# Attention of the first four units with float32 products, and ten products for each norm

## The chip, the cores and the metric

The kernel runs on one core of a Trainium2 chip. A core has five engines that run beside each other and wait for one another by semaphores: TensorE (PE, matrix products; its weight loads are listed as PEld), VectorE (DVE), ScalarE (ACT), GpSimd (POOL) and SyncE (SP, which issues the transfers). The metric is the time of one execution on the device in microseconds (us); of several runs the median is given.

## The reference

Attention over 4 batches of 8 heads with 576 positions and 64 columns, mixed with the read of a memory, then two feed-forward blocks over 2304 tokens of 512 columns:

```python
scores = scale * np.matmul(q, k.transpose(0, 1, 3, 2))   # causal mask, softmax -> a
local = np.matmul(a, v)
q_p = phi(q)                                             # x + 1 above 0, exp(x) below
mem_ret = np.einsum('bhsd,bhde->bhse', q_p, M_prev)
mem_norm = np.einsum('bhsd,bhd->bhs', q_p, z_prev)[..., None] + 1e-06
x = g * mem_ret / mem_norm + (1 - g) * local             # g from beta
x = silu(x @ moe_w_in) @ moe_w_out                       # 512 -> 2048 -> 512
h = x @ moe2_w_in                                        # 512 -> 1024
solu = h * softmax(h)
out = (layer norm of solu, times g_ln) @ moe2_w_out      # 1024 -> 512
```

All inputs are float32, and the result has to be near float32.

## The kernel before

Products are made with the type float32r (F32R), which keeps fewer bits. So every operand is split in two parts, a high one (a cast) and a low one (what the cast left off), and a product is a sum of three: high by high, low by high, high by low. ACT makes the casts, DVE or POOL subtracts for the low parts.

The work is cut into 16 units, each a pair of heads of one batch; units 0 to 3 (u < NN = 4) are batch 0. A unit goes through these steps, each a function:

- load_qk, split_both (units 0 to 3) or load_head, split_head (the others): q and k come in as rawqk; split_both makes qkh and qkl of them.
- scores: nine tiles t for a unit, 0 to 3 for the first head, 5 to 8 for the second, 4 for the last 64 queries of both. For units 0 to 3 a tile takes three products into pss: qkh by qkh, qkl by qkh, qkh by qkl.
- softmax_max (DVE, into a and nm), softmax_exp (ACT), transposes (PE, into pst).
- t_hi and t_lo: pst is written to SBUF as aTh (ACT, a cast) and aTl (DVE, a subtraction). Both are one buffer for all units.
- load_v, split_v: V comes as rawv and is split into vhl, for each head the high part beside the low part (128 columns).
- av: for each head and stretch of queries, products of vhl with aTh and aTl by key block kb into psav; the two halves of psav are added (ACT copies one into xs, DVE adds the other). The last key block has 64 rows.
- load_m, phi: the memory (rawm) is split into mh, phi of q (phe) into phh and phl. norm makes psn, 3 products for each 128 queries, so 15 for a unit of 576, and rn from it; mem makes psm with three products and y. products and spread (psr) lay factors out, finish puts the unit's output into x (POOL).

Units 0 to 3 are done in two turns each, first queries 0 to 255 of all four, then 256 to 575 of all four; the others in one turn of 576. Between them the kernel loads and decodes six chunks of feed-forward weights (load_w: twelve pieces, each a transfer wraw into a single buffer, then ACT, three DVE instructions wf, an ACT cast and a POOL subtraction into w), and it fills PE with the feed-forward work of finished batches (fill_h into psh, fill_y into psfy). The rest of the first block (psh, psy) and the second (psh, pso) follow.

The order is not that of the code. Every call is recorded with a due position (DUE, T_1, T_2, T_0), and plan (lines 240 to 313) plays them through with a table of costs (length, lines 209 to 238) and puts out one order for all engines; issue then gives the instructions in that order, so nearly all of them have line 358 in a profile, and one goes by the names of the tiles. While PE would stand idle in the first 100 us of that play, transposes of the identity named warm are put in (idle, line 1076). Buffers come from rings (p1 to p4 hold 1 to 4 buffers for a tag): a new tile of a tag waits until the one that many before it is finished.

## Time and profile before

| | |
|---|---|
| time before, median of 3 runs | 965.91 us (958.58 to 969.98) |
| the profiled execution: its own time | 966.33 us |
| its span, from the first to the last instruction | 964.5 us |
| mean granted clock of TensorE | 0.977 of full |
| PE busy | 912.0 us, 95% |
| DVE busy | 631.1 us, 65% |
| ACT busy | 508.3 us, 53% |
| POOL busy | 436.6 us, 45% |

The profile is of one execution. An engine is busy while it runs an instruction; matrix products are pipelined, and their ends are modelled, so their durations overlap and a busy PE need not be at its peak. What a product costs in a row of many is best read from the time of the whole row, divided by their number. The chain of waits follows the work that ended last back from the end, at each step to what released it. "issue" in it is time in which an engine waited for nothing that the profile shows.

### The profile page before, as it was taken

Reading aid. Unit: us, or ns where it says so; the run is one execution under the profiler, and the core shown is the slowest. Engines: PE = TensorE matmul, PEld = TensorE weight load, DVE = VectorE, ACT = ScalarE, POOL = GpSimd, SP = SyncE. Lnnn points to the kernel's source line nnn. Section 1 sums busy time; section 2 is a strip of 40 time slices with the busy share of each in tenths; the row PEclk is TensorE's granted clock in tenths of the full one; section 3 lists DMA queues with packets and bytes.
Section 4 is the critical chain, followed back from the end, with each engine's and each line's share of the span. In section 5 each row is a group of like instructions: output and inputs, shape, how many; then the busy total and the mean of one; then the engine's idle time right before and its main releaser. Section 6 shows DMA issues by size and latency. Waiting matters only on the chain.

```text
span 964.5 us, 16266 instructions
## 1 busy us (share of the span) xinstructions
PE 912.0 (95%) x5956; PEld 837.5 (87%) x5956; DVE 631.1 (65%) x1448; ACT 508.3 (53%) x1221; POOL 436.6 (45%) x366
## 2 busy tenths in 40 slices
PE   7889889999999999999978999799899999999998
PEld 5668779998999999999878999799898888888886
DVE  6887886886877675715698323953536766666663
ACT  5655578986877776745555324443434233333322
POOL 5865688776876755433454123442533211111100
PEclk9987799999999999999999999999999999999999
DMA  4433344333333221045434201320000000000000
GB/s 116 132 103 99 117 136 153 96 118 127 105 103 92 95 85 34 7 151 235 133 119 135 68 1 28 113 80 1 1 1 1 12 23 23 22 23 23 22 22 34
DMA packets 26655, 72.00 MB, mean 75 GB/s; under 512 B 3152, under 2 KB 10064, under 8 KB 25680
## 3 DMA queue, kind: packets, MB, share of 16 engines
q1 hardware_dynamic: 26576, 70.97, 22.9%
q8 instruction: 47, 0.77, 0.4%
q14 instruction: 32, 0.26, 0.1%
HBM read 60.34 MB, written 10.62 MB: 74 GB/s over the span
## 4 chain that ended last, share of the span: by engine, by line
PE 71%; DVE 17%; ACT 4%; issue 4%; DMA 2%; POOL 1%; SPq 0%; ACTq 0%; DVEq 0%; POOLq 0%
PE psh L358 24%; PE psy L358 10%; PE pso L358 10%; DVE wf L358 8%; PE psav L358 6%; PE psfy L358 6%; PE pst L358 5%; PE pss L358 5%; PE psr L358 2%; PE psn L358 2%; DMA wraw<-in_w 2%; DVE aTl L358 1%; ACT wf L358 1%; DVE phe L358 1%; PE psm L358 1%
## 5 line engine op out<-in xcount | busy, mean ns | idle before, releaser
L358 PE MATMUL psh<-xh,w 128*128 128x288 f32 (+2 forms) x1024 | 203.8, 299 | 2.6 <-ACT w L358 1.7
L358 PEld LDWEIGHTS psh<-xh,w 128*128 128x128 f32 x1024 | 160.8, 189 | 4.3 <-ACT w L358 1.9
L358 POOL TENSOR_TENSOR xl<-x,xh 128x1152 fp32r<-128x1152 f32 (+3 forms) x35 | 88.2, 2522 | 115.5 <-ACT xh L358 108.5
L358 PE MATMUL psh<-xl,w 128*128 128x288 f32 (+2 forms) x512 | 139.8, 301 | 0.0
L358 DVE TENSOR_TENSOR glo<-psh,gh 128x288 fp32r<-128x288 f32 (+2 forms) x128 | 57.7, 452 | 123.3 <-ACT gh L358 123.0
L358 PE MATMUL psy<-gh,w 128*128 128x288 f32 x736 | 117.7, 298 | 8.1 <-DVE y L358 4.7
L358 PEld LDWEIGHTS psy<-gh,w 128*128 128x128 f32 x736 | 104.6, 189 | 11.4 <-ACT gh L358 4.2
L358 POOL TENSOR_TENSOR w<-wf,w 128x512 fp32r<-128x512 f32 x48 | 66.9, 1395 | 94.9 <-ACT w L358 94.7
L358 PE MATMUL pso<-w,tb 128*128 128x512 f32 x432 | 104.0, 397 | 0.0
L358 ACT ACTIVATE a<-a,nm 128x128 f32<-128x128 f32 (+4 forms) x144 | 84.4, 588 | 24.2 <-DVE nm L358 22.2
L358 PEld LDWEIGHTS pso<-w,tb 128*128 128x128 f32 x432 | 79.9, 188 | 17.2
L358 PEld LDWEIGHTS psh<-xl,w 128*128 128x128 f32 x512 | 92.5, 191 | 0.9 <-issue 0.8
L358 DVE SCALAR_TENSOR_TENSOR wf<-wraw,wf 128x512 uint32<-128x512 uint32 x96 | 90.9, 947 | 3.0
L358 PE MATMUL psh<-w,yh 128*128 128x512 f32 x288 | 90.2, 394 | 0.0
L358 DVE TENSOR_TENSOR aTl<-pst,aTh 128x512 fp32r<-128x512 f32 (+4 forms) x160 | 75.3, 483 | 22.0 <-ACT aTh L358 21.2
L358 DVE CUSTOM_DVE_ANT_0 a<-pss,tri 128x128 f32<-128x128 f32 (+4 forms) x144 | 67.0, 477 | 23.0 <-PE pss L358 18.8
L358 ACT CAST aTh<-pst 128x512 fp32r<-128x512 f32 (+4 forms) x160 | 65.7, 424 | 27.0 <-PE pst L358 24.4
L358 PE MATMUL pst<-ident,a 128*128 128x128 f32 (+1 forms) x400 | 72.8, 288 | 6.1 <-DVE aTl L358 4.4
L358 PE MATMUL psy<-glo,w 128*128 128x288 f32 x368 | 67.4, 298 | 11.1 <-DVE glo L358 11.0
L358 ACT ACTIVATE psh<-psh 128x288 f32<-128x288 f32 x84 | 33.1, 395 | 73.5 <-PE psh L358 73.5
L358 PE MATMUL psfy<-gh,w 128*128 128x288 f32 (+2 forms) x288 | 66.2, 311 | 1.5 <-ACT w L358 1.1
L358 PE MATMUL psav<-aTh,vhl 128*128 128x320 f32 (+4 forms) x224 | 65.8, 306 | 0.6 <-ACT aTh L358 0.5
(118 smaller groups left out, 2050.2 us busy)
## 6 DMA issues: line engine op xcount, KB each, us to landing
wraw<-in_w SPq DMA_DIRECT2D x32, 512.0 KB, 3.8
rawqk<-in_qk SPq DMA_DIRECT2D x24, 608.0 KB, 3.8
rawv<-in_vp SPq DMA_DIRECT2D x16, 320.0 KB, 3.0
...
```

Of the source, the lines that this page charges most:

```text
L358: getattr(target, method)(*[real(a) for a in args], **{k: real(v) for k, v in kw.items()})
```

## The change

For units 0 to 3 nothing is split any more. split_both passes rawqk on, and a tile of scores takes one float32 product. split_v passes rawv on: a product with V takes both heads' 128 columns at once, and one of them replaces the two with aTh and aTl. phi and mem use rawm and phe as they are, norm takes one product for each 128 queries, mem one instead of three. t_lo does nothing for these units; the one float32 copy of pst is made by ACT for tiles 0 to 4 and by DVE for 5 to 8. av then needs one ACT copy of psav and no addition.

Buffers: rawqk comes from the ring "st" of three. aTh and aTl become rings: units 0 to 3 use them by turns as two float32 buffers (named aTh and aTl by turns), from unit 4 on they are again the high and the low part. rawv of units 0 to 3 takes the tags "rawv" and "vhl" by turns, and rawm gets two buffers.

For the other units norm has ten products instead of 15: phh and phl each by four columns of mh, and DVE adds the two column pairs. The last key block is multiplied on 128 rows instead of 64 in all units; its lower rows are zeroed by an ACT copy once for each of the four buffers. The planner gets a price for float32 products, and the order is planned anew.

```diff
--- before.py
+++ after.py
@@ -222,6 +222,8 @@
             if method == "transpose":
                 return 109, 0
             m = cols(shape(args[1]))
+            if args[1].ap.dtype == F32:
+                return max(n, m) / .6, 0
             if m == 64:
                 return (n if o.offset < 64 * o.ap[0][0] else 128) / 2.4, 0
             return max(n, 2 * m) / 2.4 + 2.5, 0
@@ -510,9 +512,20 @@
 
     UP, LOW = slice(0, 64), slice(64, 128)
     first_q = {}
+    st = {}
     heads, raws, v_t, mem_t, s_t, unit, X, Xd, Yd = {}, {}, {}, {}, {}, {}, {}, {}, {}
-    aTh = p1.tile([128, 4096], F32R, name="aTh")
-    aTl = p1.tile([128, 4096], F32R, name="aTl")
+    a_t = {}
+
+    def a_of(u, n=0):
+
+
+        n = ("f", turn_of[u] % 2) if u < NN else ("r", n)
+        if n not in a_t:
+            a_t[n] = p1.tile([128, 3840], F32 if u < NN else F32R, tag=f"aT{n[1]}", name="aT" + "hl"[n[1]])
+
+            act.copy(heads_of(a_t[n])[64:128, :, 1024:1088], tri[64:128, 0:128].rearrange("p (j q) -> p j q", j=2))
+        return a_t[n]
+
 
     def early(u, q1, tag, tags):
 
@@ -523,7 +536,7 @@
 
         n = q1 - q0
         if u < NN:
-            raw = p2.tile([128, QW], F32, tag="rawqk", name="rawqk")
+            raw = p3.tile([128, QW], F32, tag="st", name="rawqk")
             if q1 < S:
                 sp.dma_start(raw[:, 0:2 * n].rearrange("p (t s) -> p t s", t=2),
                              qk[u, :, 0:2 * S].rearrange("p (t s) -> p t s", t=2)[:, :, 0:n])
@@ -546,14 +559,9 @@
 
     def split_both(u, q1):
         raw = raws.pop(u)
-        n = raw.shape[1]
-        hi = p3.tile([128, QW], F32R, tag="st", name="qkh")[:, 0:n]
-        lo = p3.tile([128, QW], F32R, tag="st", name="qkl")[:, 0:n]
-        act.copy(hi, raw)
-        pool.tensor_tensor(lo, raw, f32(hi), ALU.subtract)
-        k, q = slice(0, q1), slice(q1, n)
+        k, q = slice(0, q1), slice(q1, raw.shape[1])
         for j, r in enumerate((UP, LOW, slice(0, 128))):
-            heads[u, j] = [(hi[r, q], hi[r, k]), (lo[r, q], hi[r, k]), (hi[r, q], lo[r, k])]
+            heads[u, j] = [(raw[r, q], raw[r, k])]
 
     def split_head(u, j):
 
@@ -568,33 +576,41 @@
 
     def load_v(u, q1):
         n = (q1 + 127) // 128
-        raws["v", u] = p1.tile([128, 5, 2, 64], F32, tag="rawv", name="rawv")[:, 0:n]
+        st["v"] = st.get("v", 0) + (u < NN)
+        raws["v", u] = p1.tile([128, 5, 2, 64], F32, tag="vhl" if u < NN and st["v"] % 2 else "rawv", name="rawv")[:, 0:n]
         sp.dma_start(raws["v", u], vp[u, :, 0:n].rearrange("p c (j d) -> p c j d", j=2))
 
     def split_v(u, q1):
         raw = raws.pop(("v", u))
+        if u < NN:
+            v_t[u] = raw.rearrange("p c j d -> p c (j d)")
+            return
         vhl = p1.tile([128, 5, 2, 128], F32R, tag="vhl", name="vhl")[:, 0:(q1 + 127) // 128]
         dve.tensor_copy(vhl[:, :, :, 0:64], raw)
         pool.tensor_tensor(vhl[:, :, :, 64:128], raw, f32(vhl[:, :, :, 0:64]), ALU.subtract)
         v_t[u] = vhl
 
     def load_m(u):
-        rm = p1.tile([128, 2, 132], F32, tag="rawm", name="rawm")
+        rm = p2.tile([128, 2, 132], F32, tag="rawm", name="rawm")
         sp.dma_start(rm, mz[u // 2])
         for n in range(2):
             raws["m", u + n] = rm[:, n]
 
     def phi(u, q0, q1):
         rq, rm = raws.pop(("q", u)), raws.pop(("m", u))
-        mhl = p2.tile([128, 262], F32R, tag="mh", name="mh")
-        dve.tensor_copy(mhl[:, 0:132], rm)
-        pool.tensor_tensor(mhl[:, 132:262], rm[:, 0:130], f32(mhl[:, 0:130]), ALU.subtract)
+        if u >= NN:
+            mhl = p2.tile([128, 262], F32R, tag="mh", name="mh")
+            dve.tensor_copy(mhl[:, 0:132], rm)
+            pool.tensor_tensor(mhl[:, 132:262], rm[:, 0:130], f32(mhl[:, 0:130]), ALU.subtract)
         n = q1 - q0
         k = early(u, q1, S, [320] * NP)
         e = p1.tile([128, k], F32, tag=early(u, q1, "phe", ["g", "phe", "g", "phe"]), name="phe")[:, 0:n]
         dve.tensor_scalar(e, rq, 0.0, None, ALU.min)
         act.activation(e, e, AF.Exp)
         dve.scalar_tensor_tensor(e, rq, 0.0, e, ALU.max, ALU.add)
+        if u < NN:
+            mem_t[u] = (rm, e)
+            return
         ph = p1.tile([128, k], F32R, tag=early(u, q1, "phh", ["gh0", "gh1", "gh2", "gh3"]), name="phh")[:, 0:n]
         pl = p1.tile([128, k], F32R, tag=early(u, q1, "phl", ["gl0", "gl1", "gl2", "gl3"]), name="phl")[:, 0:n]
         dve.tensor_copy(ph, e)
@@ -632,34 +648,45 @@
 
     def norm(u, q0, q1):
 
-        mhl, ph, pl = mem_t[u]
+        of = mem_t[u]
         n = q1 - q0
         starts = [min(c, n - 128) for c in range(0, n, 128)]
         k = len(starts)
-        ps = ps_a.tile([128, 5, 2], F32, tag="av", name="psn")[:, 0:k]
+        ps = ps_a.tile([128, 5, 4], F32, tag="av", name="psn")[:, 0:k]
+        rn = p2.tile([128, 5, 2], F32, tag="rn", name="rn")[:, 0:k]
         order.chain = []
         for i, c in enumerate(starts):
             c = slice(c, c + 128)
-            for m, (x, z) in enumerate(((ph, 130), (ph, 132), (pl, 130))):
-                pe.matmul(ps[:, i], x[:, c], mhl[:, z:z + 2], start=(m == 0), stop=(m == 2))
+            if u < NN:
+                pe.matmul(ps[:, i, 0:2], of[1][:, c], of[0][:, 0:2], start=True, stop=True)
+            else:
+                pe.matmul(ps[:, i], of[1][:, c], of[0][:, 130:134], start=True, stop=False)
+                pe.matmul(ps[:, i], of[2][:, c], of[0][:, 130:134], start=False, stop=True)
         order.chain = None
-        rn = p2.tile([128, 5, 2], F32, tag="rn", name="rn")[:, 0:k]
-        dve.tensor_scalar(rn, ps, 1e-6, None, ALU.add)
+        if u < NN:
+            dve.tensor_scalar(rn, ps[:, :, 0:2], 1e-6, None, ALU.add)
+        else:
+            dve.tensor_scalar(rn, ps[:, :, 2:4], 1e-6, None, ALU.add)
+            dve.tensor_tensor(rn, ps[:, :, 0:2], rn, ALU.add)
         dve.reciprocal(rn, rn)
         g = g8[:, 2 * (u % NP):2 * (u % NP) + 2].unsqueeze(1).broadcast_to([128, k, 2])
         unit["rmb", u] = products(rn, g), None
 
     def mem(u, q0, q1):
-        mhl, ph, pl = mem_t.pop(u)
-        mh, ml = mhl[:, 2:130], mhl[:, 134:262]
+        of = mem_t.pop(u)
         rmb = unit.pop(("rmb", u))
         n = q1 - q0
         y2 = p1.tile([128, early(u, q1, S, [320] * NP)], F32, tag=early(u, q1, "y2", ["gh4", "gl4", "y2", "gh4"]), name="y2")[:, 0:n]
         for cs in cuts(n):
             ps = ps_a.tile([128, cs.stop - cs.start], F32, tag="av", name="psm")
-            pe.matmul(ps, mh, ph[:, cs], start=True, stop=False)
-            pe.matmul(ps, ml, ph[:, cs], start=False, stop=False)
-            pe.matmul(ps, mh, pl[:, cs], start=False, stop=True)
+            if u < NN:
+                pe.matmul(ps, of[0][:, 2:130], of[1][:, cs], start=True, stop=True)
+            else:
+                mhl, ph, pl = of
+                mh, ml = mhl[:, 2:130], mhl[:, 134:262]
+                pe.matmul(ps, mh, ph[:, cs], start=True, stop=False)
+                pe.matmul(ps, ml, ph[:, cs], start=False, stop=False)
+                pe.matmul(ps, mh, pl[:, cs], start=False, stop=True)
             dve.tensor_tensor(y2[:, cs], ps, rmb[:, cs], ALU.mult)
         unit["y2", u] = y2
 
@@ -735,16 +762,21 @@
         else:
             j, qb = (0, t) if t < 4 else (1, t - 5)
             o = 1920 * j + 128 * qb
-            yield (lambda w: w[:, o:o + 448 * (qb + 1)].rearrange("p (k s) -> p k s", s=448)[:, :, 0:128],
+            at = 320 * j
+            yield (lambda w: w[:, o - at:o - at + 448 * (qb + 1)].rearrange("p (k s) -> p k s", s=448)[:, :, at:at + 128],
                    tiles[0][:, 0:qb + 1, :])
 
-    def t_hi(u, t):
+    def t_hi(u, t, n):
+        turn_of[u] = n
         for to, ps in t_pairs(u, t):
-            act.copy(to(aTh), ps)
+            if u < NN and t > 4:
+                dve.tensor_copy(to(a_of(u)), ps)
+            else:
+                act.copy(to(a_of(u)), ps)
 
     def t_lo(u, t):
-        for to, ps in t_pairs(u, t):
-            dve.tensor_tensor(to(aTl), ps, f32(to(aTh)), ALU.subtract)
+        for to, ps in t_pairs(u, t) if u >= NN else ():
+            dve.tensor_tensor(to(a_of(u, 1)), ps, f32(to(a_of(u))), ALU.subtract)
         s_t.pop((u, t))
 
     def av(u, j, segs, last):
@@ -758,10 +790,15 @@
             kbs = [kb for kb in range(5) if 128 * kb < q1]
             for kb in kbs:
                 f = max(q0, 128 * kb)
-                kp = 64 if kb == 4 else 128
                 w = a_cols(j, kb, f, q1)
-                pe.matmul(ps[:, f - q0:], vhl[0:kp, kb, j, :], aTh[0:kp, w], start=(kb == 0), stop=False)
-                pe.matmul(ps[:, f - q0:], vhl[0:kp, kb, j, :], aTl[0:kp, w], start=False, stop=(kb == kbs[-1]))
+                if u < NN:
+                    pe.matmul(ps[:, f - q0:], vhl[:, kb], a_of(u)[:, w], start=(kb == 0), stop=(kb == kbs[-1]))
+                    continue
+                pe.matmul(ps[:, f - q0:], vhl[:, kb, j, :], a_of(u)[:, w], start=(kb == 0), stop=False)
+                pe.matmul(ps[:, f - q0:], vhl[:, kb, j, :], a_of(u, 1)[:, w], start=False, stop=(kb == kbs[-1]))
+            if u < NN:
+                act.copy(xs[to, q0:q1], ps[to])
+                continue
             act.copy(xs[to, q0:q1], ps[other])
             dve.tensor_tensor(xs[to, q0:q1], ps[to], xs[to, q0:q1], ALU.add)
         if last:
@@ -818,6 +855,7 @@
         else:
             turns.append((9 * u, 9, u, 0, S))
     turns.sort()
+    turn_of = {}
     fill = []
     for b, c0, c1, z0, z1 in FILL:
         fs = range(PART[b])
@@ -870,7 +908,7 @@
             call(g, g + due["max"], softmax_max, u, t)
             call(g, g + due["exp"], softmax_exp, u, t, pieces[q].index(t))
             call(g, g + due["t"], transposes, u, t)
-            call(g, g + due["hi"], t_hi, u, t)
+            call(g, g + due["hi"], t_hi, u, t, n)
             call(g, g + due["lo"], t_lo, u, t)
             if u < NN:
                 for j in range(2):
```

What this does to the order shows best at three places. On PE at the start of the program; before:

```order
L358 MATMUL pss<-qkh 128x128 x2
L358 MATMUL psn<-mh,phh 128x2
L358 MATMUL pss<-qkh,qkl 128x128
L358 MATMUL pss<-qkl,qkh 128x128
L358 MATMUL pss<-qkh,qkl 128x128
L358 MATMUL pss<-qkl,qkh 128x128
L1076 MATMUL warm<-ident 128x128 x4
L358 MATMUL pss<-qkh 128x256
```

and now:

```order
L360 MATMUL warm<-ident 128x128
L360 MATMUL pss<-rawqk 128x128 x2
L360 MATMUL pss<-rawqk 128x256 x2
L360 MATMUL pst<-ident,a 128x128 x2
L360 MATMUL psn<-rawm,phe 128x2 x2
L360 MATMUL pss<-rawqk 128x128 x2
```

The first four score tiles are four products in a row on the loaded data, where twelve on split parts stood; norm has one product for each 128 queries. Up to the last psav product of unit 3 the order of before has 702 PE instructions, 124 of them warm, that of now 430, 58 of them warm; the fill work in between is about the same (72 psh in both, 37 psfy before and 32 now).

On POOL, the first rows after the masks are made; before:

```order
L358 TENSOR_TENSOR qkl<-rawqk,qkh 128x512
L384 AFFINE_SELECT trip<-trip 64x288
L358 TENSOR_TENSOR vhl<-rawv,vhl 128x4x64
L358 TENSOR_TENSOR mh<-rawm,mh 128x130
L358 TENSOR_TENSOR phl<-phe,phh 128x256
```

and now:

```order
L360 TENSOR_TENSOR bc<-rn,g_132 128x256
L360 TENSOR_SCALAR sums<-sums 128x4
L360 TENSOR_SCALAR omg<-g_132 128x8
L360 COPY omt<-omg 64x4 x2
L360 TENSOR_TENSOR bc<-sums,omg 128x256
```

The subtractions for the low parts are gone; POOL begins with the factors of norm (bc).

On DVE, between the first unit's tiles; before (ISA is the masked maximum, then its read-out):

```order
L358 TENSOR_TENSOR aTl<-pst,aTh 128x128
L358 TENSOR_SCALAR rn<-psn 128x4
L358 RECIPROCAL rn<-rn 128x4
L358 TENSOR_SCALAR phe<-rawqk 128x256
L358 TENSOR_TENSOR aTl<-pst,aTh 128x128
L358 ISA a,nm<-pss,tri 128x128
```

and now:

```order
L360 COPY aTh<-pst 128x128
L360 TENSOR_SCALAR rn<-psn 128x4
L360 RECIPROCAL rn<-rn 128x4
L360 ISA a,nm<-pss,tri 128x128
```

Of the two subtractions for aTl one is gone, and a copy of pst stands for the other.

## Rows read from the trace of the kernel before

**Rows 1.** The page, busy us and share of the span by engine.

```profile
PE 912.0 (95%) x5956; PEld 837.5 (87%) x5956; DVE 631.1 (65%) x1448; ACT 508.3 (53%) x1221; POOL 436.6 (45%) x366
```

**Rows 2.** Stretches: length, busy PE, PEld, DVE, ACT, POOL, clock, DMA, GB/s.

```profile
0.00:138.50 138.50, 118.51 (x702) 98.42 (x702) 110.50 (x274) 85.37 (x222) 91.84 (x107) 0.89 0.38 114
138.50:413.00 274.50, 266.60 (x1965) 256.34 (x1965) 202.28 (x573) 208.24 (x550) 186.45 (x155) 0.98 0.30 93
413.00:763.00 350.00, 329.08 (x2370) 320.54 (x2370) 191.85 (x347) 154.85 (x320) 131.14 (x73) 1.00 0.22 74
763.00:964.50 201.50, 197.79 (x926) 162.22 (x923) 126.43 (x257) 59.86 (x131) 27.13 (x32) 1.00 0.07 24
```

**Rows 3.** Chain of waits, 0 to 138.5 us: shares, then pieces (start, length).

```profile
by line: PE pss L358 12.9%; DVE wf L358 12.7%; PE psav L358 12.2%; issue 6.8%; PE pst L358 5.4%; PE psfy L358 4.5%; PE warm L1076 3.7%; DVE phe L358 3.0%; PE psr L358 2.9%; DMA rawm<-in_mz 2.6%; DVE aTl L358 2.5%; PE psn L358 2.5%; PE psh L
...
5.35 1.39 DVE mh L358 x2
...
71.92 4.84 PE psav L358 x18
...
128.26 0.15 DVE mh L358
...
135.81 2.73 PE psav L358 x18
```

**Rows 4.** A short stretch of the same view as rows 2.

```profile
72.00:76.00 4.00, 4.00 (x16) 3.72 (x15) 2.15 (x5) 1.77 (x5) 0.00 (x0) 0.50 0.16 42
```

**Rows 5.** Timeline: start, length, engine, instruction [idle before, who ended it].

```profile
62.77 3.79 DVE L358 SCALAR_TENSOR_TENSOR wf<-wraw,wf 128x512 uint32<-128x512 uint32 x2
...
63.16 2.85 POOL L358 TENSOR_TENSOR xl<-x,xh 128x1024 fp32r<-128x1024 f32 x1
...
67.61 1.15 PE L358 MATMUL pst<-ident,a 128*128 128x128 f32 x7 [2.43 <-DVE aTl L358]
```

**Rows 6.** Groups of DVE, 0 to 138.5 us: busy us, mean ns | idle before.

```profile
L358 DVE SCALAR_TENSOR_TENSOR wf<-wraw,wf 128x512 uint32<-128x512 uint32 x24 | 24.2, 1007 | 0.7
L358 DVE TENSOR_TENSOR aTl<-pst,aTh 128x512 fp32r<-128x512 f32 (+4 forms) x41 | 19.1, 477 | 1.3 <-ACT aTh L358 1.1
...
L358 DVE TENSOR_TENSOR xs<-psav,xs 64x256 f32<-64x256 f32 (+1 forms) x15 | 6.8, 451 | 2.5 <-ACT xs L358 2.0
...
L358 DVE CAST mh<-rawm 128x132 fp32r<-128x132 f32 x10 | 5.6, 563 | 1.2 <-DMA rawm<-in_mz 1.2
L358 DVE CAST phh<-phe 128x256 fp32r<-128x256 f32 (+2 forms) x9 | 5.4, 596 | 0.1
...
L358 DVE CAST vhl<-rawv 128x256 fp32r<-128x256 f32 (+1 forms) x8 | 3.5, 443 | 2.6 <-PE psav L358 2.6
```

**Rows 7.** The tile wf, 0 to 140 us: shortest, median and longest ns.

```profile
L358 DVE SCALAR_TENSOR_TENSOR wf<-wraw,wf x24: 659/693/2772, 20.3 to 130.0; 128x512 uint32<-128x512 uint32 x24
```

**Rows 8.** Groups of POOL, 0 to 138.5 us.

```profile
L358 POOL TENSOR_TENSOR qkl<-rawqk,qkh 128x512 fp32r<-128x512 f32 (+1 forms) x8 | 14.3, 1791 | 13.4 <-PE pss L358 11.0 <-ACT qkh L358 2.0 <-ACT a L358 0.4
L358 POOL TENSOR_TENSOR vhl<-rawv,vhl 128x256 fp32r<-128x256 f32 (+1 forms) x8 | 9.2, 1145 | 8.7 <-DVE vhl L358 8.2 <-DVE sums L358 0.6
L358 POOL TENSOR_TENSOR phl<-phe,phh 128x256 fp32r<-128x256 f32 (+2 forms) x9 | 7.8, 868 | 1.1 <-DVE phh L358 0.9
...
L358 POOL TENSOR_TENSOR mh<-rawm,mh 128x130 fp32r<-128x130 f32 x9 | 4.7, 522 | 2.0 <-DVE mh L358 1.9
```

**Rows 9.** Groups of ACT, 0 to 138.5 us.

```profile
L358 ACT CAST aTh<-pst 128x512 fp32r<-128x512 f32 (+4 forms) x41 | 16.8, 420 | 15.2 <-PE pst L358 13.7 <-PE psn L358 0.8 <-PE psav L358 0.4
...
L358 ACT CAST qkh<-rawqk 128x512 fp32r<-128x512 f32 (+1 forms) x8 | 6.4, 799 | 3.2 <-DMA rawqk<-in_qk 3.2
```

**Rows 10.** Pieces of the chain: products in a row, of two and 288 columns.

```profile
224.39 1.57 PE psn L358 x15
...
535.78 1.60 PE psh L358 x12
```

**Rows 11.** Chain of waits, 138.5 to 413 us, shares by tile.

```profile
by line: PE psfy L358 13.7%; PE psav L358 13.6%; PE psh L358 13.5%; PE pss L358 12.3%; PE pst L358 10.3%; PE psr L358 4.9%; PE psn L358 4.7%; DVE aTl L358 3.5%; PE psm L358 3.4%; DVE a L358 2.8%; DVE phe L358 2.8%; issue 2.5%; DVE xs L358 2
```

## Prediction

> **What bounds the kernel now.** I read the page's engine line first: PE is busy 912 of 964.5 us [rows 1], so nothing else can be the bound over the whole span. Then I read the busy time by stretch [rows 2], because an average hides stages. The stretches are mine: 0 to 138.5 us is the attention of units 0 to 3 (the end is that of unit 3's last psav product, 135.81 + 2.73 us, in [rows 3]), 138.5 to 413 the other twelve units with the fill work, 413 to 763 the first feed-forward block, and the rest the second. From 138.5 us on PE is busy 266.6 of 274.5, 329.1 of 350 and 197.8 of 201.5 us: there PE is the bound. In the first stretch it is not. PE is busy 118.5 of 138.5 us, but at a mean clock of 0.89, and part of its products are the filler transposes named warm (3.7% of the chain below). DVE is busy 110.5, POOL 91.8 and ACT 85.4 us, which is nearly all that chained engines can do.
>
> The chain of waits of the first stretch [rows 3] says the same. Scores (pss) have 12.9% and the products with V (psav) 12.2% of it, but DVE's weight decoding (wf) has 12.7%, "issue" 6.8%, and PE's filler 3.7%. Two rows show why PE loses time there. At 63.16 us POOL starts a 2.85 us subtraction, and DVE's two wf instructions, begun at 62.77 us, end only after it, 3.79 us together; PE then stands 2.43 us until DVE has written aTl [rows 5]. Undisturbed, one such wf instruction takes 0.66 to 0.69 us, at worst 2.77 us [rows 7]. After the stop PE runs at half clock: 0.50 granted from 72 to 76 us [rows 4], the lower of its two levels (1.2 of 2.4 GHz), and the 18 psav products take 4.84 us, where 18 of the same kind take 2.73 us later [rows 3].
>
> **What the change takes away in the first stretch.** The split parts of units 0 to 3 go. On DVE [rows 6]: aTl 40 of 41 instructions, 18.6 us; xs 6.8; mh 8 of 10, 4.5; phh 8 of 9, 4.8; vhl 3.5. That is 38.2 us. DVE gains 16 copies of pst (four tiles for each unit, those with t above 4); nothing of before copies pst on DVE, the nearest row is aTl with the same tiles, 0.477 us, so +7.6. Net DVE is 110.5 - 30.6 = 79.9 us. On POOL [rows 8]: qkl 14.3, vhl 9.2, phl 8 of 9, 6.9, mh 8 of 9, 4.2: 34.6 us less, 57.2 left. On ACT [rows 9]: qkh 6.4, and 16 of 41 aTh casts at 0.420, 6.7: 13.1 less. Four small copies of zeros come in, at most an aTh cast each, +1.7. Net 74 us.
>
> **What the float32 products cost.** Count columns for one unit, from the code. Scores: 3136 columns, three products each before, one after. V: 3200 columns, two products before, one after (both heads share it). Memory read (psm): 576 columns, three before, one after. Norm: 15 products of two columns before, five after. A split product of 288 columns costs 1.60 / 12 = 0.133 us, and one of two columns 1.57 / 15 = 0.105 us [rows 10]. Four units before: scores 17.4, V 11.8, psm 3.2, norm 6.3, together 38.7 us. No product of before has float32 operands except transposes, so I bound it. From below: one pass like a split product, 5.8 + 5.9 + 1.1 + 2.1 = 14.9 us. From above: the four products of the high and low halves of both operands, 23.2 + 23.7 + 4.3 + 8.4 = 59.6 us. I take the upper end, since a full product has to carry all four pairs, and before already needed three of them: +20.9 us of PE work. The Trainium skill (FP8 and Floating Point Precision, TensorE Precision Notes) says that true float32 takes four passes through the array, the halves against each other; no run here shows it yet, and by it the sum would be this upper end.
>
> **What of it reaches the end.** Two readings bound the first stretch. First, the old chain with the old pieces. Scores and V hold 17.9 + 16.9 = 34.8 us of it; at full clock their float32 form takes 46.9, so +12.1. The pieces of removed instructions go: 26 of them, from mh at 5.35 to mh at 128.26 us, 14.2 us in all [rows 3]. The wf pieces, 17.6 us, are stretched: twenty-four at 0.69 us would take 16.6 instead of 24.2 us [rows 6, 7]; POOL's work falls by 38%, so about 0.38 of that 7.6, 2.9 us. Norm has 2.5%, 3.5 us; if it keeps 5 of 15 products at four times the price, nothing changes. Sum +12.1 - 14.2 - 2.9 = -5: 133.5 us. This reading lets no other wait shrink. Second, the load: if DVE stays busy 80% of the stretch (110.5 / 138.5), 79.9 us of it need 100 us: -38.5. PE's issue work would still fit there, though closely: the other products up to that point (the program's order has 138 transposes, 72 psh, 37 psfy and 14 scores of unit 4, 261) at 0.105 to 0.133 us are about 30 us, so some 90 with the 59.6.
>
> I take -20, just short of the middle (-22). For more than the first reading speaks that PE's stops have the same cause as DVE's stretching, POOL holding DVE up, and that each stop costs twice, by the wait and by the half clock after it. Against the second speaks that DVE, PE and ACT then carry 80, 90 and 74 us, so none has slack to hide the others' waits. What is late next is the weight decoding: 12 pieces on a single buffer, 11.5 us each so far.
>
> **The other twelve units.** Norm falls from 15 products to ten, 60 fewer at 0.105 us: 6.3 us of PE. In that stretch the chain holds norm for 4.7% of 274.5 us, 12.9 us [rows 11]; a third of it is 4.3. I take -5. One small DVE addition for each unit comes in; DVE is busy 202 of 274.5 us there, and it lies beside PE. The last key block on 128 rows instead of 64 changes no column count; a product of two columns costs hardly less than one of 288 [rows 10], so I take nothing; if each of the 48 products lost as much as 0.05 us, it were 2.4. The later stretches run the same instructions, and their length shifts only with the weights' arrival.
>
> **Sum.** 964.5 - 20 - 5 = 939.5 us of span. The profiled execution took 966.33 us, 1.8 more than its span, so 941; the median of the runs, 965.91, is within 0.5 us of that execution, so no correction.
>
> **The rivals.** (a) *Nothing comes of it but the norm.* The weight pieces set the stretch: each passes DMA, ACT, DVE and back to the one buffer, and fill needs all 12 at the end of the stretch. For it: wf is 12.7% of the chain. Against it: the two longer of a piece's three DVE instructions take 2 x 0.69 us when quiet [rows 7], not 11.5 us; the rest is waiting in queues that the change shortens. 966.3 - 5 - (0 to 5) = 956 to 961. (b) *The whole load falls through.* The stretch shrinks to 100 us, PE keeps its clock: 966.3 - 38.5 - 6 = 922. For it: the half clock disappears if PE stands less. Against it: three engines are then about equally full. (c) *Slower: the float32 weights are loaded in front of the products.* A product of two columns costs 0.105 us although it streams almost nothing, so that is the load [rows 10]. If a float32 operand needs four such loads and none lies under the columns of the product before, each of the 96 score and V products costs 0.42 us more, 40 us, all on the chain: -5 + 40 - 5 = +30, 996 us. The Trainium skill (TensorE: Matmul & The Clock Gate, Weight-path perf modes) says that the fast weight load is not used for float32, which is what such a loss would come from; no float32 product of before shows it. It decides from (20 + 5 + 9.7) / 96 = 0.36 us unhidden for each product. Against it: the loads of before overlap (LDWEIGHTS has its own row, PEld, busy 98.4 us beside PE's 118.5 in the first stretch [rows 2]), and most float32 products would stream 0.4 us or more.
>
> **How the numbers follow.** Forecast (about 930 to 953) 0.52; (b) 0.22; (a) 0.18; (c) 0.08. Runs of before lie between 958.58 and 969.98 us, so 1% is about what can be told from no change. Faster by over 1% (below 956): forecast and (b), 0.74. Within 1%: (a), 0.18. Slower: (c), 0.08. The range leaves out (c) and the far end of (b): 918 to 962; the forecast's own is 930 to 953. The single pass as the lower bound of price lies inside it, since PE is not what the first stretch waits for.
>
> **What would show it.** Unit 3's last psav product ends near 118 us instead of 138.5; DVE is busy near 80 and POOL near 57 us up to there; the granted clock of the stretch is above 0.89. A float32 product of 512 columns stands on PE for about 0.93 us. Ten psn products of one unit take about 1.05 us. The stretch from there to the end is some 5 us shorter than 826 us. I am wrong if the first stretch is over 130 us with DVE at 80 us (then waits, not load, set it), or if PE's products of 128 columns take much over 0.24 us (then (c)).

## The result, and the profile after

| | before | after |
|---|---|---|
| time, median | 967.86 us (958.58 to 969.98) | 925.86 us (925.15 to 928.34) |
| profiled execution: time, span | 966.33, 964.5 us | 926.01, 923.2 us |
| mean granted clock | 0.977 | 0.996 |
| unit 3's last psav product ends at | 138.5 us | 110.8 us |
| from there to unit 15's last psav product | 273.8 us | 258.2 us |
| from there to the end | 552.2 us | 554.2 us |

After is to before as 0.9599, 95% interval 0.9554 to 0.9644: 42 us less, where 25 were forecast. 925.86 lies inside the range (918 to 962), but below the forecast's own (930 to 953): the range held because it reached down to rival (b), not because the sum did. The stretches are cut at the same two products as in [rows 2], so they compare although the order is another: 27.7 us went in the first stretch, 15.6 in the second, 2.0 came back behind it. Comparisons leave disturbed executions out; of the first experiment, norm_only, the profiled execution was such a one (span 1079.6 us at a clock of 0.754), so none of its trace is read, and its median, 957.7 us over all ten executions, is 954.5 over the seven that are left.

The page's line of engines, which answers to [rows 1]:

```profile
PE 880.5 (95%) x5762; PEld 801.8 (87%) x5762; DVE 593.7 (64%) x1396; ACT 495.8 (54%) x1201; POOL 401.8 (44%) x334
```

The busy time by stretch, as in [rows 2]:

```profile
0.00:110.83 110.83, 99.13 (x555) 74.35 (x556) 76.16 (x209) 73.20 (x198) 58.50 (x76) 1.00 0.47 145
110.83:369.00 258.17, 252.44 (x1914) 242.70 (x1912) 198.00 (x584) 207.14 (x552) 185.49 (x153) 1.00 0.31 98
369.00:723.00 354.00, 332.69 (x2383) 323.89 (x2383) 194.52 (x351) 157.06 (x324) 132.07 (x75) 0.99 0.21 73
723.00:923.20 200.20, 196.28 (x916) 160.91 (x915) 125.06 (x254) 58.37 (x128) 25.76 (x30) 1.00 0.07 24
```

In the first stretch DVE is busy 76.2 us and POOL 58.5, near the 79.9 and 57.2 of the prediction. PE is busy 99.1 instead of 118.5 us and idle 11.7 instead of 20, and its clock is full where it was 0.89. The same view over 10 us shows the place of the stop in [rows 4], first before, then after:

```profile
70.00:80.00 10.00, 10.00 (x35) 8.43 (x35) 5.66 (x14) 5.27 (x13) 2.28 (x2) 0.50 0.16 53
```

```profile
70.00:80.00 10.00, 9.95 (x60) 7.86 (x58) 6.21 (x20) 8.42 (x20) 5.95 (x8) 1.00 0.55 193
```

At half clock (1.2 of 2.4 GHz) PE was fully busy for 10 us and made 35 products; a busy share says nothing of the work done. A mean of 0.89 over 138.5 us is 2 x 0.11 x 138.5 = 30 us at the lower level, and they cost PE 15 us of time (an estimate, as PE is nearly always busy in them). The same reading in steps of 1 us gives 15.4 us for the first stretch of before and 5.1 for its second, in three short spells; after, there is no half clock in either. Behind them it cost 2.3 us before and 4.5 after, about the 2.0 us that came back.

The chain of waits of the first stretch, which answers to [rows 3], and a group and the tile of DVE, to [rows 6, 7]:

```profile
by line: DVE wf L360 17.0%; PE psav L360 13.7%; PE pss L360 11.2%; issue 7.4%; PE pst L360 4.8%; DVE a L360 4.4%; DMA rawq<-in_qt 4.3%; PE warm L1114 3.8%; DMA wraw<-in_w 3.6%; DVE phe L360 3.0%; PE psh L360 2.7%; ACT a L360 2.6%; DMA rawqk
...
59.69 0.56 PE psn L360 x6
...
89.21 4.27 PE psav L360 x20
```

```profile
L360 DVE SCALAR_TENSOR_TENSOR wf<-wraw,wf 128x512 uint32<-128x512 uint32 x24 | 20.7, 863 | 0.8
```

```profile
L360 DVE SCALAR_TENSOR_TENSOR wf<-wraw,wf x24: 686/693/1796, 17.9 to 105.1; 128x512 uint32<-128x512 uint32 x24
```

Ten products of one norm, in the chain of the second stretch:

```profile
303.45 1.01 PE psn L360 x10
```

Every float32 product has two records. So x20 are the ten products with V of one unit's second turn, 2 x (3 x 320 + 192 + 64) = 2432 columns: 4.27 / 2432 = 1.76 ns a column, which makes 0.90 us for 512. A split product has 0.133 / 288 = 0.46 ns a column [rows 10]; float32 costs 3.8 times that. The Trainium skill (FP8 and Floating Point Precision, TensorE Precision Notes) gives four passes, and this trace agrees. A piece of wf fell from 1007 to 863 ns, its longest from 2772 to 1796.

These products with V stand on 128 rows. Most scores work on 64 rows, and there the price is another; one score of 128 columns and one of 512 on PE, each two records, with what comes behind it:

```profile
14.37 0.49 PE L360 MATMUL pss<-rawqk 64*128 64x128 f32 x2
14.78 0.70 PE L360 MATMUL psm<-phe,rawm 128*128 128x256 f32 x2
...
85.57 1.12 PE L360 MATMUL pss<-rawqk 64*128 64x512 f32 x2
86.62 0.98 PE L360 MATMUL pst<-ident,a 128*128 128x128 f32 x7
```

From start to start these are 0.41 us for 128 columns, where 1.76 ns a column gives 0.23, and 1.05 for 512 (0.93 forecast).

What no step of the prediction had stands in the timeline of PE (start, length, engine, instruction) at the last key block of one head, first before, then after:

```profile
303.60 0.28 PE L358 MATMUL psav<-aTl,vhl 128*128 128x192 f32 x1
303.80 0.29 PE L358 MATMUL psav<-aTh,vhl 64*128 64x64 f32 x1
303.94 0.27 PE L358 MATMUL psav<-aTl,vhl 64*128 64x64 f32 x1
304.14 0.40 PE L358 MATMUL psm<-phh,mh 128*128 128x288 f32 x1
```

```profile
267.62 0.27 PE L360 MATMUL psav<-aTl,vhl 128*128 128x192 f32 x1
267.74 0.22 PE L360 MATMUL psav<-aTh,vhl 128*128 128x64 f32 x1
267.79 0.28 PE L360 MATMUL psav<-aTl,vhl 128*128 128x64 f32 x1
267.90 0.43 PE L360 MATMUL pst<-ident,a 128*128 128x128 f32 x2
```

From the start of the product ahead of the pair to the start of the one behind it lie 0.54 us before and 0.28 after: the pair on 64 rows starts 0.20 us late, and what comes behind it 0.20 us late again. The weight loads (PEld) of the same places say why:

```profile
303.51 0.19 PEld L358 LDWEIGHTS psav<-aTl,vhl 128*128 128x128 f32 x1
303.80 0.18 PEld L358 LDWEIGHTS psav<-aTh,vhl 64*128 64x128 f32 x1
303.91 0.19 PEld L358 LDWEIGHTS psav<-aTl,vhl 64*128 64x128 f32 x1
304.14 0.30 PEld L358 LDWEIGHTS psm<-phh,mh 128*128 128x128 f32 x2
```

```profile
267.54 0.19 PEld L360 LDWEIGHTS psav<-aTl,vhl 128*128 128x128 f32 x1
267.65 0.19 PEld L360 LDWEIGHTS psav<-aTh,vhl 128*128 128x128 f32 x1
267.76 0.19 PEld L360 LDWEIGHTS psav<-aTl,vhl 128*128 128x128 f32 x1
267.89 0.20 PEld L360 LDWEIGHTS pst<-ident,a 128*128 128x128 f32 x2
```

A load on 128 rows starts under the product before it (267.65, its product at 267.74). That on 64 rows behind products on 128, and that on 128 behind 64, start only with their own product (303.80 and 304.14).

### The profile page after: what moved, and what is told of

It reads as the page before. It is cut to its first block, busy times and chain, and to the rows that moved or that the text cites. A ratio compares the mean times of both kernels' runs of the same rounds, so it can differ in the third digit from the quotient of the medians.

```text
span 923.2 us, 15757 instructions
## 1 busy us (share of the span) xinstructions
PE 880.5 (95%) x5762; PEld 801.8 (87%) x5762; DVE 593.7 (64%) x1396; ACT 495.8 (54%) x1201; POOL 401.8 (44%) x334
## 4 chain that ended last, share of the span: by engine, by line
PE 68%; DVE 18%; ACT 6%; issue 4%; DMA 3%; POOL 0%; ACTq 0%; DVEq 0%; SPq 0%
PE psh L360 24%; PE pso L360 11%; PE psy L360 11%; DVE wf L360 9%; PE pst L360 5%; PE psav L360 5%; PE pss L360 5%; PE psfy L360 5%; DMA wraw<-in_w 2%; DVE phe L360 2%; DVE a L360 1%; DVE aTl L360 1%; PE psr L360 1%; ACT wf L360 1%; PE psm L360 1%
## 5 line engine op out<-in xcount | busy, mean ns | idle before, releaser
L360 PE MATMUL psh<-xl,w 128*128 128x288 f32 (+2 forms) x512 | 137.2, 299 | 0.0
L360 PEld LDWEIGHTS pso<-w,tb 128*128 128x128 f32 x432 | 79.9, 188 | 17.2
L360 DVE SCALAR_TENSOR_TENSOR wf<-wraw,wf 128x512 uint32<-128x512 uint32 x96 | 86.7, 903 | 3.1
L360 DVE CUSTOM_DVE_ANT_0 a<-pss,tri 128x128 f32<-128x128 f32 (+4 forms) x144 | 67.6, 476 | 21.3 <-PE pss L360 17.4
L360 PE MATMUL psy<-glo,w 128*128 128x288 f32 x368 | 68.3, 301 | 12.2 <-DVE glo L360 12.1
L360 PE MATMUL pst<-ident,a 128*128 128x128 f32 (+1 forms) x400 | 70.2, 280 | 5.0 <-ACT rb L360 2.1
L360 DVE TENSOR_TENSOR aTl<-pst,aTh 128x128 fp32r<-128x128 f32 (+3 forms) x120 | 56.2, 484 | 18.6 <-ACT aTh L360 18.2
L360 PEld LDWEIGHTS psy<-glo,w 128*128 128x128 f32 x368 | 55.5, 191 | 14.0 <-DVE glo L360 14.0
L360 PE MATMUL psfy<-gh,w 128*128 128x288 f32 (+2 forms) x288 | 63.6, 303 | 1.8 <-ACT w L360 1.7
L360 PEld LDWEIGHTS psh<-w,yh 128*128 128x128 f32 x288 | 53.9, 188 | 11.9
```

The costliest lines, as they stand in the source:

```text
L360: getattr(target, method)(*[real(a) for a in args], **{k: real(v) for k, v in kw.items()})
```

## The experiments

"First stretch" is up to unit 3's last psav product, "second" from there to unit 15's. The changed kernel was not measured again beside the experiments; the kernel before was, and its medians (966.63, 966.13 and 966.83 us) lie within 2 us of the one above. What the half clock costs a stretch is read as above, in steps of 1 us, half of the time at the lower level. Each row below is of the busy time by stretch, its columns as in [rows 2].

### The two parts apart: norm_only, f32_only

norm_only is the kernel before with ten products for each norm from unit 4 on; f32_only is the changed kernel with the norm of 15 products:

```diff
-                pe.matmul(ps[:, i], of[1][:, c], of[0][:, 130:134], start=True, stop=False)
-                pe.matmul(ps[:, i], of[2][:, c], of[0][:, 130:134], start=False, stop=True)
+                for m, (x, z) in enumerate(((of[1], 130), (of[1], 132), (of[2], 130))):
+                    pe.matmul(ps[:, i, 0:2], x[:, c], of[0][:, z:z + 2], start=(m == 0), stop=(m == 2))
```

> The kernel before with nothing but the ten products for each norm in units 4 to 15; the order is planned anew. The changed kernel ran 13.6 us less after unit 3's last psav product, where 5 were forecast for the norm. Theory N (the whole surplus is the norm's): 952 to 956 us, 12 to 14 below before. Theory R (the norm saves its 60 products of 0.105 us, 4 to 6 us, and the rest is given by the first stretch, which hands over more finished work or a steadier clock): 960 to 963 us.

> The changed kernel with 15 products for each norm in units 4 to 15, as before; the float32 products of units 0 to 3 stay. Theory N: 12 to 14 us slower than the changed kernel, 938 to 940 us. Theory R: 4 to 6.5 us slower, 930 to 932.5 us, and the stretch after unit 3's last psav product is still 7 to 9 us shorter than in the kernel before.

Measured: norm_only 954.5 us, 0.9884 of before (0.9835 to 0.9934), 6 to 16 us less. That median lies in Theory N's range, but it scatters too much to part the two. f32_only 933.4 us, 0.9678 of before (0.9604 to 0.9751), 7.5 us more than the changed kernel, 0.9 us above Theory R's range and 4.6 below Theory N's. Its second stretch, and a part of it:

```profile
111.30:377.00 265.70, 260.10 (x1971) 251.30 (x1969) 198.47 (x572) 208.22 (x552) 186.33 (x153) 0.99 0.30 95
...
137.00:141.00 4.00, 4.00 (x18) 3.92 (x19) 2.56 (x10) 2.98 (x8) 4.00 (x4) 0.57 0.48 156
```

The second stretch is 7.5 us longer than the changed kernel's; the first is nearly the same (111.3 us). But a spell at half clock from 137 us, which the changed kernel's trace lacks, holds up to 1.7 of the 7.5 us, so the norm is worth 5.8 us or a little more. The runs say the same: the one execution of f32_only at a mean clock of 0.996 took 931.32 us, 5.7 more than the changed kernel's two at 0.996 (926.01, 925.15). Why norm_only gains more, 12 us, is open: its order is another. The rest of the change alone takes 0.0322 of the time, and it still shortens the second stretch from 273.8 to 265.7 us (Theory R: 7 to 9), 8.1 us that the prediction has nowhere.

### The last key block on 64 rows again: kp64

```diff
+                kp = 64 if kb == 4 and u >= NN else 128
-                pe.matmul(ps[:, f - q0:], vhl[:, kb, j, :], a_of(u)[:, w], start=(kb == 0), stop=False)
+                pe.matmul(ps[:, f - q0:], vhl[0:kp, kb, j, :], a_of(u)[0:kp, w], start=(kb == 0), stop=False)
```

> The changed kernel, but from unit 4 on the last key block is multiplied on 64 rows again, as before the change. Theory K: the weight load of a 64-row product does not start under the 128-row product ahead of it. In the trace of before one pair of last-block products takes 0.54 us from the start of the product ahead of it to the start of the one behind (302.54+1.06 = 303.60 to 304.14), in that of the changed kernel 0.28 (267.62 to 267.90). 24 pairs (units 4 to 15, two heads) at 0.26 us are 6.2 us: 932 us, all of it between unit 3's and unit 15's last psav product (258.2 there becomes about 264.5), and 64-row loads stand at the start of their products. Rival N, the step as predicted (the rows cost nothing, and what the second stretch gained beyond the norm comes from the clock, 0.98 before and 1.00 after): 925 to 927.5 us.

Measured: 930.27 us (929.36 to 931.59), 4.4 us more than the changed kernel.

```profile
111.60:375.50 263.90, 259.09 (x1912) 247.40 (x1911) 197.63 (x584) 207.31 (x553) 185.48 (x153) 0.99 0.30 96
...
212.00:217.00 5.00, 5.00 (x30) 4.94 (x30) 3.50 (x12) 3.79 (x9) 4.28 (x3) 0.66 0.42 106
```

The second stretch lasts 263.9 instead of 258.2 us, 5.7 more, with the same number of records within two; the first ends at 111.6. Up to 1.7 us of the 5.7 are a spell at half clock, from 212 us. The late starts are back:

```profile
272.23 0.28 PE L360 MATMUL psav<-aTl,vhl 128*128 128x192 f32 x1
272.44 0.29 PE L360 MATMUL psav<-aTh,vhl 64*128 64x64 f32 x1
272.57 0.27 PE L360 MATMUL psav<-aTl,vhl 64*128 64x64 f32 x1
272.77 0.44 PE L360 MATMUL pst<-ident,a 128*128 128x128 f32 x2
```

Theory K holds: 0.54 us for the pair, as before, and so for all 24 pairs. The 6.2 us that they lose by the timeline come out as 4.0 in the stretch without the half clock, 4.4 by the median. The second stretch's 15.6 us are then 5.8 for the norm, 4.0 for the rows and up to 5.1 for the half clock of before, 14.9 together (an estimate).

### The removed loads put back, planned anew: pool_back, dve_back

Both are the changed kernel with instructions that nobody's result needs: POOL subtracts in the sizes that the change took from it (27.9 us more in the first stretch), or DVE subtracts every tile of pst of units 0 to 3 (13.5 us more).

```diff
+            if u < NN:
+                scrap = p2.tile([128, S], F32, tag="kl", name="scrap")[0:ps.shape[0], 0:int(np.prod(ps.shape[1:]))]
...
+                dve.tensor_tensor(scrap, ps, to(a_of(u)), ALU.subtract)
```

> The changed kernel with POOL given back subtractions of the sizes of the removed ones for units 0 to 3 (on rawqk, rawv, rawm and phe), written to buffers that nobody reads; no product waits for them. Theory A (of the prediction: POOL's instructions hold DVE up, PE stops for DVE and then runs at half clock): DVE's wf instructions are stretched again to a mean of 0.9 us or more, the clock of the first stretch falls below 1.00, and the time is 8 to 15 us above the changed kernel. Theory B (it was the work on DVE itself and the waits of products for their low parts, not POOL's hold on DVE): within 3 us of the changed kernel.

> The changed kernel with DVE given back the 40 subtractions of aTl's sizes for units 0 to 3 (pst minus its copy, into a buffer that nobody reads), 19 us of DVE work; they hold pst as long as before, but no product waits for them. Theory A: DVE then carries about 95 us in a first stretch of 110.8, so it grows by some 5 us. Theory B (DVE's load was what set the stretch): 10 to 19 us above the changed kernel, DVE busy over 85% of the stretch.

Measured: pool_back 939.77 us (+13.9 over the changed kernel), dve_back 941.41 (+15.5). pool_back, then dve_back:

```profile
0.00:118.30 118.30, 103.47 (x565) 78.65 (x565) 76.26 (x207) 72.24 (x196) 86.36 (x115) 0.96 0.43 134
118.30:381.60 263.30, 252.96 (x1914) 243.29 (x1912) 203.34 (x587) 208.49 (x554) 187.55 (x154) 1.00 0.30 97
```

```profile
0.00:118.00 118.00, 107.02 (x588) 79.42 (x588) 89.67 (x245) 73.12 (x195) 58.09 (x75) 1.00 0.43 130
118.00:382.90 264.90, 254.51 (x1896) 243.71 (x1893) 205.44 (x588) 209.50 (x556) 186.97 (x154) 0.99 0.31 98
```

pool_back bears all the marks of Theory A: a mean of wf of 910 ns, a clock of 0.96, 13.9 us. dve_back has the time of Theory B, but DVE is busy 76% of its stretch and not 85%. So neither theory alone holds; both loads matter. But the second stretch, in which nothing was added, is 5 to 7 us longer too (3.4 of dve_back's 6.7 are half clock, none of pool_back's), and the records in the first are other in number (565 and 588 against 555): the planner counts the new instructions and puts out another order. So these two don't price a load alone.

### The same loads, the order kept: pool_same_order, dve_same_order, both_same_order

Here the extra instructions are put in behind the planner, so that everything else on every engine comes in the changed kernel's order:

```diff
             getattr(target, method)(*[real(a) for a in args], **{k: real(v) for k, v in kw.items()})
+            for more in self.extra.get(i, ()):
+                more(real)
...
+    def more_pool(x):
+        for a in range(0, x.shape[1], free):
+            b = min(a + free, x.shape[1])
+            order.extra.setdefault(len(order.ops) - 1, []).append(
+                lambda real, x=x[:, a:b], n=b - a: nc.gpsimd.tensor_tensor(real(scrap[:, 0:n]), real(x), real(x), ALU.subtract))
```

> The changed kernel with POOL subtractions of the removed sizes (rawqk, rawv, rawm and phe of units 0 to 3 against themselves, into 320 columns of scratch that nobody reads, about 35 us), put in behind the planner, so that the order of every other instruction on every engine stays that of the changed kernel. The earlier run with this load was planned anew and was 13.9 us longer: its first stretch ended at 118.3 instead of 110.8 us, and its second lasted 263.3 instead of 258.2. Theory L (the load itself, by buffers held longer and by DVE slowed): the first stretch ends at 117 to 120, the second keeps 258 to 260, 932 to 936. Theory R (the new plan made those 13.9 us, the load lies beside PE): first stretch under 114, 925.5 to 929.

> The changed kernel with one DVE subtraction of pst for each tile of units 0 to 3 (the removed aTl, into scratch that nobody reads, 18.4 us and some 0.07 for each of ten more cuts), put in behind the planner, so that the order of every other instruction stays. The earlier run with this load, planned anew, was 15.5 us longer (first stretch 118.0, second 264.9). Theory L (the load itself): first stretch 116 to 119, second 258 to 260, 931 to 936. Theory R (the new plan): first stretch under 114, 925.5 to 929.

> Both loads of the two runs beside this one together, the order of all other instructions that of the changed kernel (POOL in cuts of 192 columns, DVE of 128, so about 4 us more on each than there). Theory L, the loads add up: the sum of both runs' gains over the changed kernel and up to 4 us more, about +14 to +20, clock over 0.97 in the first stretch. Theory C, PE's stops bring the half clock back as in the kernel before (0.89 there): more than the sum of the two by over 5 us, clock under 0.95 up to unit 3's last psav product.

Measured: 936.92 us (+11.1), 940.75 (+14.9) and 958.4 (+32.5, 0.9913 of before). In this order:

```profile
0.00:122.10 122.10, 104.95 (x557) 78.23 (x558) 78.85 (x209) 73.43 (x199) 96.16 (x140) 0.96 0.43 132
122.10:379.90 257.80, 251.97 (x1911) 242.51 (x1910) 198.26 (x584) 207.00 (x552) 185.53 (x153) 1.00 0.31 98
```

```profile
0.00:127.10 127.10, 108.05 (x557) 78.95 (x558) 94.14 (x269) 74.47 (x199) 58.76 (x76) 0.93 0.40 125
127.10:385.00 257.90, 252.03 (x1913) 242.58 (x1912) 198.46 (x584) 206.96 (x552) 185.47 (x153) 1.00 0.31 99
```

```profile
0.00:144.20 144.20, 118.31 (x557) 85.29 (x558) 100.32 (x309) 74.05 (x198) 97.37 (x160) 0.87 0.35 111
144.20:402.90 258.70, 252.42 (x1913) 242.67 (x1911) 198.89 (x585) 207.38 (x554) 185.59 (x153) 1.00 0.31 98
```

Theory L holds for the single loads: all of it lies in the first stretch, and the second keeps its 258 us. 37.7 us on POOL cost 11.3 us of the stretch, 0.30 for each; 18.0 us on DVE cost 16.3, 0.91 for each. With POOL's load DVE itself is 2.7 us busier over the same 209 instructions (78.85 against 76.16). The Trainium skill (SBUF — State Buffer, SBUF: two separate sides) has the two engines share a pair of ports that one of them holds for a whole instruction; the 2.7 us agree, and they are small beside the 11.3; the extra instructions also hold the buffers of rawqk and rawv longer, and the shares of the two causes weren't parted. With both the first stretch is 33.4 us longer and looks like that of the kernel before: clock 0.87 (0.89 there), PE busy 118.3 us (118.5), though PE's 557 records are nearly the 555 that took 99.1 us. So 19.2 of the 33.4 us are the same PE work at a lower clock, and 14.2 idle time. Theory C holds: the clock is under 0.95, and 33.4 us are 5.8 more than the sum of 27.6. The clock fell with each load alone too (0.96, 0.93). It cost 5.1 us with POOL's load, 8.5 with DVE's and 18.8 with both; what is left is 6.2, 7.8 and 14.6. So without the clock the loads just add up (14.0 against 14.6, though DVE has 6 us more in the run with both), and all but 0.6 of the surplus is the clock. Without it, 1 us on POOL costs 0.16 and 1 us on DVE 0.43. The mean of wf is 859 ns in the run with both loads, as in the changed kernel (863): the stretch and the clock of before come back without the slow wf instructions that the prediction started from. POOL's extra instructions there are shorter, though, than those that held wf up in before.

What PE waited for (engine, line, tile; us in total, times, longest) up to 120 us with DVE's load (a little short of its first stretch), and below it up to 110.8 us in the changed kernel:

```profile
PE pst L361 <- DVE scrap L785: 5.7, 5, 2.3
PE pss L361 <- DVE nm L361: 5.4, 8, 1.4
```

```profile
PE pss L360 <- DVE nm L360: 2.3, 4, 1.4
```

DVE holds PE up in two ways: it reads pst later, which keeps the buffer of the next transpose, and the maxima (nm) behind it are late.

### More work for PE: v_twice

Each float32 product with V of units 0 to 3 is made twice, so their attention output is about doubled; the order is planned anew.

```diff
+                    pe.matmul(ps[:, f - q0:], vhl[:, kb], a_of(u)[:, w], start=(kb == 0), stop=False)
+                    pe.matmul(ps[:, f - q0:], vhl[:, kb], a_of(u)[:, w], start=False, stop=(kb == kbs[-1]))
```

> The changed kernel, in which each float32 product with V of units 0 to 3 is made twice (so their attention output is about doubled, and is not the reference's). That is 12,800 more columns at 1.76 ns (10 products with 2432 columns took 4.27 us): 22.5 us more PE work in the first stretch, nothing more on any other engine. Theory P, PE is the bound of the first stretch now (busy 99.1 of 110.8 us): all but the old idle time shows, +18 to +23 us, 944 to 949. Theory W, the waits for DVE, ACT and the weight pieces still set it and hide half of it or more: up to +11, 926 to 937.

Measured: 944.1 us, 18.2 more than the changed kernel.

```profile
0.00:127.10 127.10, 119.46 (x641) 90.79 (x642) 73.79 (x210) 74.74 (x200) 57.67 (x76) 0.99 0.41 129
```

Theory P: 16.3 of the 22.5 us come out in the first stretch, 0.72 for each. Only 1.7 of them are half clock, so without it PE's work costs 0.65 there, more than DVE's 0.43. The planner had put 14 fewer warm and 13 fewer psfy products into the stretch, so this is not the load alone.

### One part split again: qk_split, v_split

The scores, or V and the transposed attention, of units 0 to 3 go back to split parts in the changed kernel:

```diff
+        act.copy(hi, raw)
+        pool.tensor_tensor(lo, raw, f32(hi), ALU.subtract)
-            heads[u, j] = [(raw[r, q], raw[r, k])]
+            heads[u, j] = [(hi[r, q], hi[r, k]), (lo[r, q], hi[r, k]), (hi[r, q], lo[r, k])]
```

```diff
-        for to, ps in t_pairs(u, t) if u >= NN else ():
+        for to, ps in t_pairs(u, t) if u >= 0 else ():
             dve.tensor_tensor(to(a_of(u, 1)), ps, f32(to(a_of(u))), ALU.subtract)
```

> The changed kernel with the scores of units 0 to 3 split again: qkh cast by ACT (6.4 us), qkl subtracted by POOL (14.3 us), and three products of qkh and qkl in place of one float32 product. PE: 3136 x 4 columns at 1.76 ns = 22.1 us become 17.4, so 4.7 us less. Theory L (load of POOL and ACT counts beside PE): the earlier run with 34.6 us more on POOL was 13.9 us longer, so 14.3 on POOL gives +5.7, ACT's 6.4 and its extra step before the scores +1 to 3, PE's gain -2 to -4: +3 to +7, 929 to 933. Theory P (only PE's work counts): -3 to -5, 921 to 923.

> The changed kernel with V and the transposed attention of units 0 to 3 split again (vhl, aTh and aTl, the addition into xs), scores, norm and memory read staying float32. DVE gets 18.6 + 6.8 + 3.5 us and loses 7.6 of copies, +21.3; POOL +9.2; PE's products with V cost 11.8 instead of 22.5 us, -10.7. Theory L by the slopes measured so far (18.4 us on DVE +15.5, 34.6 on POOL +13.9, 22.5 on PE +18.2, planned anew each): +18 + 3.7 - 8.7 = +13, 936 to 942. Theory P (only PE's work counts): -8.7, 916 to 920.

Measured: qk_split 938.66 us (+12.8), v_split 942.64 (+16.8), both past the upper end of Theory L (v_split by 0.6 us), and on the other side from Theory P. The first stretch of qk_split, then of v_split:

```profile
0.00:116.80 116.80, 109.23 (x598) 85.13 (x599) 74.96 (x203) 76.78 (x201) 66.86 (x82) 0.94 0.42 129
```

```profile
0.00:128.00 128.00, 111.80 (x627) 85.98 (x628) 96.77 (x258) 81.35 (x217) 69.22 (x84) 0.93 0.42 129
```

Each part of the float32 change pays in these orders. Splitting V again puts DVE at 96.8 us and gives 17.2 us back in the first stretch, 8.5 of them half clock. Of qk_split's 12.8 us only 6 lie in the first stretch, and the half clock costs it 6.8 us there and as much in the second, so its loss is no more than the clock's. Both were planned anew, so their totals hold a part of unknown size that is the order's.

### Two buffers for the weight pieces: two_wraw

```diff
-            raw = temp.tile([128, 512, 2], U32, tag="wraw", name="wraw")
+            raw = temp.tile([128, 512, 2], U32, tag="rawqk" if temp is p2 else "wraw", name="wraw")
-            call(z, ws[0][0] + DUE["w"], load_w, ws[0][2], w0p, p1, (ws[0][1],), least=least)
+            call(z, ws[0][0] + DUE["w"], load_w, ws[0][2], w0p, p2, (ws[0][1],), least=least)
```

> The changed kernel, in which the twelve weight pieces of the first stretch have two buffers for wraw and for wf instead of one. Theory W (the weight pieces, DVE wf 17.0% and the transfer wraw 3.6% of the first stretch's chain, hold it up): the transfers come out from between the pieces, 3.6% of 110.8 = 4 us and a little of wf: 918 to 922.5. Theory P (PE is the bound, the pieces lie beside it): 923.5 to 928.

Measured: 935.49 us, 9.6 more than the changed kernel, which neither theory has.

```profile
0.00:117.40 117.40, 104.89 (x533) 76.67 (x534) 77.79 (x207) 73.09 (x198) 57.77 (x76) 0.91 0.44 137
```

The timeline of DVE shows what two buffers do (the last piece starts here at 74.30 us, in the changed kernel at 102.72):

```profile
27.20 0.59 DVE L360 TENSOR_SCALAR wf<-wf 128x512 uint32<-128x512 uint32 x1 [0.38 <-ACT wf L360]
...
30.80 2.37 DVE L360 SCALAR_TENSOR_TENSOR wf<-wraw,wf 128x512 uint32<-128x512 uint32 x2
```

The pieces come in pairs, almost 6 us of DVE in a row, and far ahead of their use; the clock is 0.91. That the pairs made the stops is not shown, since this order is another too. The pieces are done 28 us earlier, and the stretch still ends 6.6 us later. But the half clock costs it 10.2 us; at full clock it would end some 3.6 us earlier than the changed kernel's (an estimate), about Theory W's 4 us. So the early pieces don't pay as they stand, and whether they hold the stretch stays open. No version tried is faster than the changed kernel.

## Why the prediction was right, point by point

**The bound of the first stretch: right.** DVE and POOL, and PE's stops, set it. The loads came out as summed (76.2 and 58.5 us against 79.9 and 57.2), and putting both back (both_same_order) brings back the stretch, the clock and PE's busy time of before. That POOL works on PE by holding DVE up is only in part so: its load made DVE 2.7 us busier, and with both loads wf was not slower.

**The price of float32 products: right; that of the split products: too low.** On 128 rows 1.76 ns a column against 1.85 (4 x 0.133 / 288). On two columns it was too high: six records, three products, took 0.56 us, 0.19 each, where four times 0.105 is 0.42. On 64 rows it was too low, 0.41 us for 128 columns. Counted on PE from each start to the next, without idle time and with half clock taken as half, the products of units 0 to 3 (pss, psav, psm, psn) take 25.7 + 23.6 + 4.1 + 4.7 = 58 us after, near the 59.6 of the prediction, and 22.9 + 17.4 + 4.5 + 7.4 = 52 us before, where it had 38.7 from the price of products in a row on 128 rows. So PE had 6 us more to do, not 20.9 (an estimate).

**What reaches the end: right in kind, short in size, -27.7 for -20.** The step that failed is the choice between two readings. The first, -5, took only scores and V at full clock, for +12.1, and let no other wait shrink. The text named the half clock after a stop as a reason to go beyond it, but gave it no price. It had one: 30 us at half clock, 15 us of PE's time, all of it gone after. PE's rows of before and after account for the rest: 8 us less idle, and 4 less of work at full clock (66 fewer warm products, 9 us, against 6 for the dearer products and 1 less elsewhere). The measured slopes give too much: DVE's 34.3 us less at 0.91 are 31, POOL's 33.3 at 0.30 are 10, PE's 6 us more at 0.72 are +4, together -37; without the clock -15, -5 and +4, and with its 15 us -31. These sums are estimates, and the loads put back were not the removed ones instruction by instruction.

**The norm: near, about -6 for -5.** Ten products take 1.01 us in a row (1.05 forecast), so 60 fewer at 0.105 make 6.3; f32_only gives 5.8 without its spell at half clock, 7.5 with it. Taking a third of the chain's share, 4.3, as the lower end was too careful where PE is busy 97% of the time.

**The last key block: wrong.** "A product of two columns costs hardly less than one of 288, so I take nothing" looked at the length of products alone and bounded the edit on the loss side only. The edit changes when the next weights are loaded: 0.26 us for each of 24 pairs, 6.2 us by the timeline, 4.0 to 5.7 in kp64's stretch, 4.4 by its median. The timeline of before had shown it, in a gap of 0.20 us in front of a product of 64 columns.

**The clock of the second stretch: not priced.** [rows 2] has it at 0.98 there; the 5.1 us that this cost went as well.

**The sum.** First stretch 27.7, norm 5.8, rows 4.0 and the second stretch's clock 5.1 make 42.6 us; 2.0 came back behind it, and the span fell by 41.3. Some 18 us of that are the clock (15.4 + 5.1 - 2.2); the mean clocks of the table say the same, 0.023 x 964.5 = 22 against 0.004 x 923.2 = 4.

**The rivals.** (a) is refuted: f32_only, without the norm, is 33 us under before. Whether the weight pieces hold the first stretch of the changed kernel is another question, which two_wraw leaves open. (b) had a time within 4 us of the result and one right mark, the full clock, but not its mechanism: the first stretch ended at 110.8, between its 100 and the forecast's 118, and the rest came from the second stretch. PE, busy 99.1 of 110.8 us, left hardly room for 100, and v_twice shows that its work counts there. (c) is refuted: the ten products cost 1.76 ns a column with their loads, so nothing of those shows. On 64 rows there is a loss of its kind, 0.15 to 0.2 us a product, but all scores together take 25.7 us where 1.76 ns a column makes 22.1: 4 us and not 40.

**The signs.** Clock, DVE, POOL and the ten psn products came as given. The 512 columns took 1.05 us for 0.93. One sign of being wrong came too: 128 columns much over 0.24 us, 0.41 for a score on 64 rows; with V, on 128 rows, they take 0.22. Unit 3's last psav product was 7 us earlier than 118, and the remainder was shorter by 13.6 us (826.0 to 812.4), not 5: 6 for the norm, 4 for the rows, 3 for the clock.
